# Portions of weight decoding, first turns and stored weight pairs in a three-stage kernel

## The chip, the cores and the metric

One Trainium2 chip, one of its cores. The metric is the device time of one execution in microseconds; lower is better.

## The reference

`x` is 2 x 3008 x 256; the weights come in float64, x in float32. Three stages follow each other:

```python
X = np.fft.fft(np.fft.fft(x, axis=1), axis=2).real      # 2 x 3008 x 256
x = X.reshape(6016, 256)
h = x @ w_in; x = (h * sigmoid(h)) @ w_out              # d_ff = 2048
h = x @ w_in2; y = (h * clip(h + 3, 0, 6) / 6) @ w_out2
```

## The kernel before, in words

**Transform.** The real part of the transform is computed once for each pair of tokens k and -k, as three matmul steps per group g (g0 to g11): `step1` on the loaded x (lines 269 to 284), `step2` (lines 299 to 318; ScalarE L312 or VectorE L314 adds a term, ScalarE L317 takes the rest), `step3` (lines 320 to 328), then `evacuate` (ScalarE L338 writes `eo`). PSUM tiles of steps 2 and 3 have two buffers each.

**Units.** Layer one works on 6 chunks of 502 token pairs (`CHUNKS`), and on 16 blocks f of 128 hidden units; layer two on 12 chunks (`tch`) and 8 pairs of blocks. A unit is one chunk with one f (layer one) or one pair (layer two). The list `units` (lines 423 to 430) has 96 units of layer one, u0 to u95, and 96 of layer two, u96 to u191. Layer one runs in two turns: in the first, chunk j takes f from 0 to PARTS[j]-1, in the second the rest; the sum of the first turn is kept in `y1` and added to. Before, the first turns are 4, 6, 8, 9, 10, 11 units (u0 to u47). Layer two runs pairs 0 to 3 for chunks 0 to 3 (u96 to u111), then pairs 4 to 7 for these (u112 to u127), then all 8 for the others.

**One unit of layer one.** float32 products are made of three matmuls each (`mm3`, lines 229 to 232: hi*hi, lo*hi, hi*lo, 502 columns each). `win1` does 6 matmuls into the PSUM tile `ab` (two buffers), then three VectorE instructions make h (L460, L463, L464); `parts` runs two ScalarE activations (L473, L474); `low` subtracts on GpSimd (L530); `wout1` does 12 matmuls into four accumulators, three units later (LAG = 3). After the last f of a turn the accumulators are copied (L552 on ScalarE, L554 on VectorE) or added (four L556 on VectorE) to `y1`.

**One unit of layer two.** `win2` does 12 matmuls; ScalarE L519, VectorE L520, ScalarE L471, VectorE L530; `wout2` does 12 matmuls; results by L580/L582.

**Order.** Every engine takes its instructions in the order in which the program issues them, so what is issued ahead stands in the queue of its engine, and its waits hold all that is behind it. The loop at lines 588 to 626 issues, for unit i: win(i), low(i-1), wout(i-3), the pending `lo` subtractions (`do_later`, L147), parts(i), results, decoding steps (`spare`), the split of the next chunk (L146 on ScalarE; its L147 follows one unit later).

**Decoding.** The weights come as float64 bit patterns, in groups of two blocks: 8 pairs for each layer, "pair g" here. For one pair: load (1 MB, SP's queue), magnitude (ScalarE L98), five bit steps on VectorE (L104, L106, L110, L114, L116), for layer one four more (L168, L170, L172, L174), for layer two one sum (L183), then hi on ScalarE (L161) and lo on VectorE (L163). It is a generator that yields each step's cost in credit (680, 680, 1200, 680, 1200; 680, 680, 420, 420; 1200; 1200), or PAUSE behind load, magnitude and L161. `advance(steps, ns)` adds ns to the credit and issues steps while the credit is over 0; at a PAUSE it returns and keeps the credit. `drive` issues steps at once when `win1` or `win2` needs a pair that isn't done. Pairs 0 to STAGED-1 of layer two are decoded within layer one, stored to DRAM (`store_w2`, L188), and loaded and split from unit `turn` on (`load_w2`, `split_w2`), into the buffers of layer-one pairs that are used up.

Of the kernel before, what the change touches and what calls it, by code (L numbers as in the profile page):

```python
# [59 lines left out]
XCH += [(1, 0, 3), (1, 3, 4), (1, 7, 4), (1, 11, 4), (1, 15, 2)]  # L60
QA = NA + 1

PARTS = (4, 6, 8, 9, 10, 11)
TURNS = 4
LAG = 3
EARLY = 2
STAGED = 3
PAUSE = -1


def body(tc, xh, x128, t1, t2, t3, w1, w128, w2, out):
    nc = tc.nc
    V, A, T, G = nc.vector, nc.scalar, nc.tensor, nc.gpsimd
# [9 lines left out]
    eo = eop.tile([P, 2, NPAIR], F32, name="eo")  # L83
    w2_d = [dr.tile([P, 2, 512], F32, name=f"w2_d{g}", tag=f"w2_d{g}") for g in range(STAGED)]
    e128_d = [dr.tile([1, n], F32, name=f"e128_d{j}", tag=f"e128_d{j}") for j, (_, n) in enumerate(CHUNKS)]
# [33 lines left out]
    def decoder(key, src, finish, first=0, end=NF // 2, pools=()):  # L119

        for g in range(first, end):
            if g >= first + len(pools):
                load_raw(key, src, g)
                yield PAUSE
            a = dp.tile([P, 2, 512], F32, name="da", tag="da")
            raw = raws.pop((key, g))
            if g < first + len(pools):
                if g == first:
                    ts = [q.tile([P, 2, 512], F32, name="dt", tag="dt") for q in pools]
                    magnitude(raw, ts[0])  # L130
                    yield PAUSE
                t = ts[g - first]
            else:
                t = dp.tile([P, 2, 512], F32, name="dt", tag="dt")
                magnitude(raw, t)
                yield PAUSE
            yield from bits_to_float32(raw, t, a)
            if g + 1 < first + len(pools):
                magnitude(raws[key, g + 1], ts[g + 1 - first])
            yield from finish(g, t, a)  # L140
# [59 lines left out]
    def decode_w128(raw):  # L200
        t, a = (dp.tile([P, NF], F32, name=n, tag=n) for n in ("w128t", "w128a"))
        magnitude(raw, t)
        yield PAUSE
        for _ in bits_to_float32(raw, t, a):
            yield 70
        V.tensor_tensor(out=w128_sb, in0=a, in1=t, op=ALU.add)
        yield 70

    credit = [0]

    def advance(steps, ns):
        credit[0] += ns
        while credit[0] > 0:
            took = next(steps, None)
            if took is None:
                credit[0] = 0
            elif took == PAUSE:
                return
            else:
                credit[0] -= took  # L220
# [78 lines left out]
    def step2(g):  # L299
        n, t = divmod(g, 6)  # L300
        ps = psA.tile([P, 2, 256], F32, name="ps2", tag="s2")
        o2 = fft.tile([P, 2, 256], F32, name="o2", tag="o2", bufs=3)
        for i in range(2):
            q = 4 * (2 * t + i)
            e, o = (out1[n][:, h, q : q + 4].rearrange("p q s j -> p (q s j)") for h in range(2))
            T.matmul(ps[:, i, 0:129], e, t2_sb[:, 0:129], start=True, stop=True)
            T.matmul(ps[:, i, 129:256], o, t2_sb[:, 129:256], start=True, stop=True)

        x128 = xr[:, n, 2 * t : 2 * t + 2]
        if g < 6:  # L310
            for i in range(2):
                A.activation(o2[:, i, 0:129], ps[:, i, 0:129], AF.Identity, bias=x128[:, i : i + 1])  # L312
        else:
            V.tensor_tensor(  # L314
                out=o2[:, :, 0:129], in0=ps[:, :, 0:129], in1=x128.unsqueeze(2).to_broadcast([P, 2, 129]), op=ALU.add
            )
        A.activation(o2[:, :, 129:256], ps[:, :, 129:256], AF.Copy)  # L317
        return o2
# [28 lines left out]
    nx = len(XCH)  # L347
    for i in range(4):
        load_x(i)
    nc.sync.dma_start(xl, x128)  # L350
    steps = itertools.chain(
        decode_w128(w128_raw), decoder(1, w1, finish_w1, pools=(fft, dp)), decoder(2, w2, store_w2, 0, STAGED)
    )
    steps2 = decoder(2, w2, finish_w2, STAGED)
    o2, full, done = {}, {}, 0
    folded = fold(0)
    i = g = 0
    busy(8)

    def step1_next():  # L360

        nonlocal folded, i
        x = folded
        if i + 4 < nx:
            load_x(i + 4)
        if i + 1 < nx:
            folded = fold(i + 1)
        step1(i, x)
        i += 1
        if i == 1:  # L370
            nc.sync.dma_start(t2_sb, t2)
            nc.sync.dma_start(t3_sb, t3)
            nc.sync.dma_start(w128_raw, w128)
        if i < 5:
            busy(3)
        if i == 5:
            step1_last()
        if i == nx - 4:
            load_raw(1, w1, 0, fft)
            load_raw(1, w1, 1)  # L380
            advance(steps, 1)
        if i == nx - 3:
            advance(steps, 400)

    def steps23(g):
        nonlocal done
        if g < 12:
            o2[g] = step2(g)
        if 0 <= g - 1 < 12:
            full[g - 1] = step3(o2.pop(g - 1))  # L390
        if 0 <= g - 2 < 12:
            done = evacuate(g - 2, full.pop(g - 2))
# [3 lines left out]
    while i < nx:  # L396
        steps23(g)
        g += 1
        step1_next()
        do_later()  # L400
        if i >= nx - 1:
            advance(steps, 3000)
    xp.release()
    psX.release()

# [18 lines left out]
    tch = [(2 * c + s * n, n) for c, n in CHUNKS for s in range(2)]  # L424
    segs = [(1, j, range(p * q, (p, NF)[q])) for q in (0, 1) for j, p in enumerate(PARTS)]
    last1 = len(segs) - 1
# [1 line left out]
    segs += [(2, j, range(half)) for j in range(TURNS, len(tch))]  # L428
    units = [(k, f) for k, (_, _, fs) in enumerate(segs) for f in fs]
    n1 = NF * len(CHUNKS)  # L430
    turn = n1 - 10

    gs = {}

# [7 lines left out]
        ghi = pools[0].tile([P, 2, CHUNK], F32R, name="ghi", tag="ghi", bufs=4)  # L442
        return ps, h, ghi

    def spare(times=1):
        if k <= last1:
            advance(steps, 300 * times)
        else:
            advance(steps2, 800 * times)

    def win1(k, f):
        n = size(k)
# [28 lines left out]
    while g < 14:  # L481
        steps23(g)
        if g >= 12:
            k, f = units[g - 12]
            gs[k, f] = win1(k, f)
            parts(k, f)
        do_later()
        if g == 8:
            xs[0] = split_eo(0)
        advance(steps, 1500)  # L490
        g += 1
    fft.release()
    psA.release()
# [15 lines left out]
    def win2(k, f):  # L509
        n = size(k)  # L510
        hi, lo = xs[k]
        while f >= STAGED and len(finished) <= NF + 2 * (f - STAGED):
            drive(steps2)
# [24 lines left out]
    def wout1(k, f):  # L538
        _, j, fs = segs[k]
        c, n = CHUNKS[j]  # L540
        hi, lo = gs.pop((k, f))
        y, first, last = accumulators(f, fs, ["y00", "y01", "y10", "y11"])
        for m in range(2):
            wh, wl = w(1, f, 256 + 128 * m)
            for s in range(2):
                mm3(y[2 * m + s][:, :n], wh, wl, hi[:, s, :n], lo[:, s, :n], first, last)
        if last:
            for m in range(2):
                for s in range(2):
                    dst, src = y1[:, m, 2 * c + s * n : 2 * c + (s + 1) * n], y[2 * m + s][:, :n]  # L550
                    if fs[0] == 0 and m == 0:
                        A.activation(dst, src, AF.Copy)  # L552
                    elif fs[0] == 0:
                        V.tensor_copy(dst, src)  # L554
                    else:
                        V.tensor_tensor(out=dst, in0=dst, in1=src, op=ALU.add)  # L556

# [30 lines left out]
    for i in range(len(units) + LAG):  # L588
        if i < len(units):
            k, f = units[i]  # L590
            layer, j, fs = segs[k]
            
            if i >= EARLY:
                gs[k, f] = (win1 if layer == 1 else win2)(k, f)
        if 1 <= i <= len(units):
            low(*units[i - 1])
        if i >= LAG:
            k_, f_ = units[i - LAG]
            (wout1 if segs[k_][0] == 1 else wout2)(k_, f_)
        do_later()  # L600
        if EARLY <= i < len(units):
            parts(k, f)
        while unhurried:
            unhurried.pop(0)()
        if i >= len(units):
            continue
        if layer == 2:
            spare(3)
        if f == fs[len(fs) // 2 - 1] and k + 1 < len(segs):
            l_, j_, _ = segs[k + 1]  # L610
            xs[k + 1] = split_eo(j_) if l_ == 1 else split_y(j_)
        if 3 <= i < turn:
            spare(3)
        elif i < n1:

            if i == turn:
                for _ in steps:
                    pass
                load_w2(0)
            g, odd = divmod(i - turn, 2)  # L620
            if odd and 0 < g < STAGED:
                load_w2(g)
            elif not odd and 0 < g <= STAGED:
                split_w2(g - 1)
            elif g > STAGED:
                advance(steps2, 1)
    for p in (pools[1], psB, pools[0], xsp, eop, yp, dr, dp, wp, per):
        p.release()
# [133 lines left out]
```

## Time and profile before

| | before |
|---|---|
| median of 3 runs | 1023.1 us (1020.49 to 1024.23) |
| the profiled execution | 1024.39 us, span 1022.6 us |
| TensorE busy | 982.6 us, 96% |
| VectorE / ScalarE / GpSimd busy | 657.9 / 505.8 / 236.2 us |
| mean granted clock of TensorE | 0.983 |
| DMA | 39.41 MB, mean 39 GB/s |

Times within the span count from its start. Busy time of TensorE is of pipelined matmuls with modelled ends, so a busy TensorE is not one at its peak: what shows how full a stretch is, is the number of matmuls in it.

### The profile page before, as it was taken

The page shows a single profiled execution, that of the slowest core. Times are in us where ns is not written, and L with a number is a line of the kernel's source. Part 1 is how long each engine was busy: PE and PEld are TensorE (multiplying, and loading weights), DVE is VectorE, ACT ScalarE, POOL GpSimd, SP SyncE. Part 2 cuts the span into 40 slices and gives each one's busy share as a digit, 9 for nine tenths or more (in the row PEclk, how much of TensorE's full clock was granted, in tenths as well). Part 3 has the DMA queues.
Part 4 walks back from the last instruction along what each step waited for, and adds up shares of the span by engine and source line. Part 5 has one row for each costly group of instructions (what it writes and reads, how often), then busy time and mean ns, then how long its engine had stood idle before and what let it go on. Part 6 is the DMA issues. An engine that isn't in the chain of part 4 may idle for free.

```text
span 1022.6 us, 10956 instructions
## 1 busy us (share of the span) xinstructions
PE 982.6 (96%) x4416; PEld 812.2 (79%) x4416; DVE 657.9 (64%) x738; ACT 505.8 (49%) x543; POOL 236.2 (23%) x101
## 2 busy tenths in 40 slices
PE   8869999999998999998999899999999999999998
PEld 7847878888887888886777688888888888888887
DVE  7787978988888876678577655454444344344443
ACT  3646556665654555565245444443444434344442
POOL 0025555666555565552000000000000000000000
PEclk9988999999999999999899899999999999999999
DMA  9311110110110210012021001000000000000000
GB/s 357 126 39 49 52 38 25 42 51 1 52 62 2 71 31 31 11 42 83 1 82 42 1 1 40 21 21 1 21 1 21 21 1 20 1 21 21 1 21 20
DMA packets 10719, 39.41 MB, mean 39 GB/s; under 512 B 1318, under 2 KB 6316, under 8 KB 7852
## 3 DMA queue, kind: packets, MB, share of 16 engines
q1 hardware_dynamic: 10524, 38.44, 10.6%
q8 instruction: 34, 0.56, 0.2%
q10 hardware_dynamic: 144, 0.27, 0.1%
q14 instruction: 17, 0.14, 0.0%
HBM read 30.96 MB, written 7.75 MB: 38 GB/s over the span
## 4 chain that ended last, share of the span: by engine, by line
PE 77%; DVE 14%; ACT 4%; issue 3%; DMA 1%; POOL 0%; ACTq 0%; DVEq 0%
PE y L230 14%; PE y L232 14%; PE y L231 14%; PE ab L232 11%; PE ab L231 11%; PE ab L230 11%; DVE h L520 2%; DVE da L110 1%; ACT h L519 1%; DMA x<-in_xh 1%; DVE h L460 1%; DVE h L463 1%; DVE dt L104 1%; DVE dt L116 1%; ACT ghi L473 1%
## 5 line engine op out<-in xcount | busy, mean ns | idle before, releaser
L230 PE MATMUL y<-ghi,whi 128*128 128x502 f32 (+1 forms) x768 | 302.5, 394 | 2.1 <-DVE y L556 2.1
L232 PE MATMUL y<-ghi,wlo 128*128 128x502 f32 (+1 forms) x768 | 301.9, 393 | 0.0
L231 PE MATMUL y<-glo,whi 128*128 128x502 f32 (+1 forms) x768 | 301.4, 392 | 0.3 <-POOL glo L530 0.3
L530 POOL TENSOR_TENSOR glo<-h,ghi 128x1004 fp32r<-128x1004 f32 (+1 forms) x96 | 235.8, 2457 | 235.5 <-ACT h L474 221.8
L520 DVE SCALAR_TENSOR_TENSOR h<-h,ab 128x1004 f32<-128x1004 f32 (+1 forms) x96 | 115.1, 1199 | 265.2 <-ACT h L519 265.0
L473 ACT ACTIVATE ghi<-h 128x1004 fp32r<-128x1004 f32 (+1 forms) x96 | 100.2, 1044 | 167.9 <-DVE h L464 165.4
L519 ACT ACTIVATE h<-ab,three 128x1004 f32<-128x1004 f32 (+1 forms) x96 | 105.4, 1097 | 156.7 <-PE ab L232 147.6
L230 PEld LDWEIGHTS y<-ghi,whi 128*128 128x128 f32 x768 | 146.6, 191 | 33.9 <-issue 2.8
L231 PEld LDWEIGHTS y<-glo,whi 128*128 128x128 f32 x768 | 146.9, 191 | 31.8 <-POOL glo L530 0.6
L232 PEld LDWEIGHTS y<-ghi,wlo 128*128 128x128 f32 x768 | 145.8, 190 | 30.4
L471 ACT ACTIVATE ghi<-h 128x1004 fp32r<-128x1004 f32 (+1 forms) x96 | 100.3, 1045 | 122.1 <-DVE h L520 122.1
L230 PE MATMUL ab<-uhi,whi 128*128 128x502 f32 (+1 forms) x384 | 152.5, 397 | 8.1 <-DVE h L520 5.8
L232 PE MATMUL ab<-uhi,wlo 128*128 128x502 f32 (+1 forms) x384 | 152.5, 397 | 3.0 <-DVE wlo L163 3.0
L231 PE MATMUL ab<-ulo,whi 128*128 128x502 f32 (+1 forms) x384 | 151.9, 396 | 1.7 <-DVE ulo L147 1.7
L530 DVE TENSOR_TENSOR glo<-h,ghi 128x1004 fp32r<-128x1004 f32 (+1 forms) x96 | 114.9, 1196 | 0.0
L460 DVE SCALAR_TENSOR_TENSOR h<-eb,w_sb,ab 128x502 f32<-128x502 f32 (+1 forms) x96 | 70.4, 734 | 66.2 <-PE ab L232 57.5
L474 ACT ACTIVATE h<-h 128x1004 f32<-128x1004 f32 (+1 forms) x96 | 100.2, 1044 | 8.7
L230 PEld LDWEIGHTS ab<-uhi,whi 128*128 128x128 f32 x384 | 73.6, 192 | 25.3 <-DVE h L520 7.1
L232 PEld LDWEIGHTS ab<-uhi,wlo 128*128 128x128 f32 x384 | 73.7, 192 | 18.7 <-DVE wlo L163 3.4
L231 PEld LDWEIGHTS ab<-ulo,whi 128*128 128x128 f32 x384 | 73.9, 192 | 17.4 <-DVE ulo L147 2.0
L230 PE MATMUL ab<-xhi,whi 128*128 128x502 f32 (+1 forms) x192 | 75.9, 395 | 8.5 <-DVE h L464 8.5
L232 PE MATMUL ab<-xhi,wlo 128*128 128x502 f32 (+1 forms) x192 | 75.8, 395 | 2.8 <-DVE wlo L163 2.8
(77 smaller groups left out, 783.9 us busy)
## 6 DMA issues: line engine op xcount, KB each, us to landing
raw<-in_w SPq DMA_DIRECT2D x16, 1024.0 KB, 4.9
x<-in_xh SPq DMA_DIRECT2D x6, 1024.0 KB, 6.9
out<-y SPq DMA_DIRECT2D x20, 251.0 KB, 2.2
eb<-e_d SPq DMA_DIRECT2D x10, 251.0 KB, 3.3
x<-in_xh SPq DMA_DIRECT2D x3, 512.0 KB
w_d<-dt SPq DMA_DIRECT2D x3, 512.0 KB, 2.9
w<-w_d SPq DMA_DIRECT2D x3, 512.0 KB, 3.3
out<-y SPq DMA_DIRECT2D x4, 250.0 KB, 2.0
```

Source lines behind the costliest of these rows:

```text
L104: V.tensor_scalar(out=t, in0=t, scalar1=2.0**-15, scalar2=None, op0=ALU.max)
L110: V.scalar_tensor_tensor(out=ai, in0=high, scalar=-0x40000000, in1=ai, op0=ALU.bitwise_and, op1=ALU.bitwise_or)
L230: T.matmul(o, wh, xhi, start=first, stop=False)
L231: T.matmul(o, wh, xlo, start=False, stop=False)
L232: T.matmul(o, wl, xhi, start=False, stop=last)
L460: V.scalar_tensor_tensor(out=h[:, 0, :n], in0=eb[:, :n], scalar=w128_sb[:, f : f + 1], in1=ab[:, 0, :n], op0=ALU.mult, op1=ALU.add)
L471: A.activation(ghi[:, :, :n], h[:, :, :n], AF.Copy)
L473: A.activation(ghi[:, :, :n], h[:, :, :n], AF.Silu)
L474: A.activation(h[:, :, :n], h[:, :, :n], AF.Silu)
L519: A.activation(h[:, :, :n], hp[:, :, :n], AF.Relu, bias=three)
L520: V.scalar_tensor_tensor(out=h[:, :, :n], in0=h[:, :, :n], scalar=6.0, in1=hp[:, :, :n], op0=ALU.min, op1=ALU.mult)
L530: eng.tensor_tensor(out=glo[:, :, :n], in0=h[:, :, :n], in1=ghi[:, :, :n], op=ALU.subtract)
```

## The change

- First turns of layer one are 4, 4, 6, 8, 10, 12 units (44 in all instead of 48).
- At a PAUSE `advance` keeps at most 400 of credit.
- What is added to the credit: 2500 and 1500 instead of 3000 twice (groups g3, g4), 1300 instead of 1500 per group g5 to g13, 1200 instead of 900 per unit up to u53 and from u2 on, 900 to u81; in layer two 2000 instead of 2400.
- STAGED is 4 instead of 3: pairs 0 to 3 of layer two are decoded and stored within layer one; loading and splitting them begins at u82 instead of u86. Decoding of the next pair starts at u94 as before.
- The four accumulators of a first turn are all copied by ScalarE.
- g6 and g7 take ScalarE's L312 instead of VectorE's L314.

```diff
-PARTS = (4, 6, 8, 9, 10, 11)
+PARTS = (4, 4, 6, 8, 10, 12)
-STAGED = 3
+STAGED = 4
@@ advance
             elif took == PAUSE:
+                credit[0] = min(credit[0], 400)
                 return
@@ step2
-        if g < 6:
+        if g < 8:
@@ transform loop
         if i >= nx - 1:
-            advance(steps, 3000)
+            advance(steps, 2500 if i < nx else 1500)
@@ units
-    turn = n1 - 10
+    turn = n1 - 14
-    def spare(times=1):
+    def spare():
         if k <= last1:
-            advance(steps, 300 * times)
+            advance(steps, 1200 if i < 54 else 900)
         else:
-            advance(steps2, 800 * times)
+            advance(steps2, 2000)
@@ groups g5 to g13
-        advance(steps, 1500)
+        advance(steps, 1300)
@@ wout1
-                    if fs[0] == 0 and m == 0:
+                    if fs[0] == 0:
                         A.activation(dst, src, AF.Copy)
-                    elif fs[0] == 0:
-                        V.tensor_copy(dst, src)
@@ main loop
-            spare(3)
+            spare()
-        if 3 <= i < turn:
-            spare(3)
+        if 2 <= i < turn:
+            spare()
-            elif g > STAGED:
+            elif g > STAGED and i >= n1 - 2:
                 advance(steps2, 1)
```

## Rows read from the trace of the kernel before

**Rows 1.** The page: busy tenths and TensorE's clock in 40 slices of the span.

```profile
PE   8869999999998999998999899999999999999998
PEclk9988999999999999999899899999999999999999
```

**Rows 2.** Busy time by window: us, then each engine (x instructions), clock, DMA share, GB/s.

```profile
151.50:303.30 151.80, 151.80 (x667) 125.56 (x666) 133.73 (x163) 90.39 (x91) 90.00 (x37) 1.00 0.11 37
595.30:704.70 109.40, 109.40 (x481) 90.47 (x480) 55.41 (x53) 46.58 (x45) 0.00 (x0) 1.00 0.05 19
```

**Rows 3.** TensorE's timeline (start, us, instruction, idle before): first matmuls of u0, u4, u96, u116.

```profile
56.17 0.47 PE L230 MATMUL ab<-xhi,whi 128*128 128x502 f32 x1
...
73.45 0.76 PE L230 MATMUL ab<-xhi,whi 128*128 128x502 f32 x1 [6.06 <-DVE h L464]
...
465.38 0.46 PE L230 MATMUL ab<-uhi,whi 128*128 128x502 f32 x1 [0.35 <-DVE h L464]
...
595.32 0.39 PE L230 MATMUL ab<-uhi,whi 128*128 128x502 f32 x1
```

**Rows 4.** TensorE's waits: for whom, us in total, times, longest.

```profile
PE ab L230 <- DVE h L464: 8.8, 5, 6.1
PE ab L230 <- DVE h L520: 5.8, 2, 3.5
PE ab L232 <- DVE wlo L163: 5.7, 3, 3.0
```

**Rows 5.** Windows, TensorE alone: us, busy (x matmuls), granted clock, DMA share, GB/s.

```profile
69.80:80.10 10.30, 6.39 (x15) 0.50 0.38 87
97.10:100.50 3.40, 3.40 (x10) 0.50 0.00 0
...
486.20:493.00 6.80, 5.39 (x13) 0.50 0.00 0
```

**Rows 6.** Timelines of VectorE and of GpSimd (last row), u0 to u2.

```profile
59.31 0.68 DVE L464 TENSOR_TENSOR h<-h,ab 128x502 f32<-128x502 f32 x1
...
63.20 1.92 DVE L104 TENSOR_SCALAR dt<-dt 128x1024 f32<-128x1024 f32 x1 [1.14 <-ACT dt L98]
...
65.88 3.36 DVE L110 SCALAR_TENSOR_TENSOR da<-raw,da 128x1024 int32<-128x1024 int32 x1
...
62.21 2.36 POOL L530 TENSOR_TENSOR glo<-h,ghi 128x1004 fp32r<-128x1004 f32 x1 [61.28 <-ACT h L474]
```

**Rows 7.** Timelines of VectorE and of ScalarE (last row), u101 to u102.

```profile
506.98 0.69 DVE L104 TENSOR_SCALAR dt<-dt 128x1024 f32<-128x1024 f32 x1
...
508.43 1.23 DVE L110 SCALAR_TENSOR_TENSOR da<-raw,da 128x1024 int32<-128x1024 int32 x1
...
511.68 1.22 DVE L183 TENSOR_TENSOR dt<-da,dt 128x1024 f32<-128x1024 f32 x1
...
512.93 1.06 ACT L161 ACTIVATE whi<-dt 128x1024 fp32r<-128x1024 f32 x1 [5.91 <-DVE dt L183]
```

**Rows 8.** Timelines of TensorE and of ScalarE (last row) in the transform.

```profile
36.39 1.06 PE L324 MATMUL ps<-t_sb,o 128*128 128x128 f32 x8
...
43.27 1.16 PE L324 MATMUL ps<-t_sb,o 128*128 128x128 f32 x8 [2.58 <-ACT eo L338]
...
41.31 1.06 ACT L161 ACTIVATE whi<-dt 128x1024 fp32r<-128x1024 f32 x1 [2.72 <-DVE dt L174]
```

**Rows 9.** Timelines of VectorE and of TensorE (last row), u7 to u8.

```profile
92.90 1.70 DVE L147 TENSOR_TENSOR xlo<-eo,xhi 128x1004 fp32r<-128x1004 f32 x1
94.52 1.21 DVE L163 TENSOR_TENSOR wlo<-dt,whi 128x1024 fp32r<-128x1024 f32 x1
...
95.78 0.49 PE L232 MATMUL ab<-xhi,wlo 128*128 128x502 f32 x1 [1.90 <-DVE wlo L163]
```

**Rows 10.** Groups by line: us in all, mean ns of one, idle before.

```profile
L554 DVE COPY y<-y 128x502 f32<-128x502 f32 (+1 forms) x12 | 7.6, 673 | 0.0
...
L552 ACT ACTIVATE y<-y 128x502 f32<-128x502 f32 (+1 forms) x12 | 6.7, 584 | 1.2 <-PE y L232 0.9
```

## The prediction

> **What bounds the kernel now.** The slices of the page come first [rows 1]: TensorE is busy in nearly every slice, and its clock dips near the start, at a third and around the middle. So the end is set by TensorE and its holes. Two windows without a hole give the pace [rows 2]: 37 units of layer one in 151.8 us are 4.10 us each (18 matmuls of 0.228), 20 units of layer two in 109.4 us are 5.47 us each (24 matmuls). Next, the starts of units on TensorE [rows 3]: u0 56.17, u4 73.45, u96 465.38, u116 595.32. Set against the pace:
>
> - u0 to u4: 17.3 us where 36 matmuls need 8.2; 9.1 lost.
> - u4 to u96: 391.9 us for 92 units, which need 377.5; 14.4 lost.
> - u96 to u116: 129.9 us for 20 units, which need 109.4; 20.5 lost.
> - u116 to the end: nothing to win.
>
> Who causes it is in the waits of TensorE [rows 4]: layer one waits for h on VectorE (up to 6.1 us at once) and for wlo, a weight pair that is finished late; layer two for h again. Each wait of about 2 us or more may be paid twice, as the clock falls to 0.5 (1.2 instead of 2.4 GHz) for 3.4 to 10 us [rows 5]: ten matmuls in 3.4 us cost 1.7 us more, thirteen in 6.8 us some 2.5.
>
> Why h is late: all five bit steps of a pair were issued in one go on gathered credit. At u1 to u2 they stand ahead of h of u2 [rows 6]: L104 takes 1.92 and L110 3.36 us, each held until GpSimd's subtraction ends, and u4 starts only after that. In layer two [rows 7], six steps from 506.98 to 512.90 hold ScalarE 5.91 us at L161, and the next L519 is queued behind it.
>
> **The change part by part.** *Portions.* I add up credits as the code does. With the cap (400) and 1200 per unit a first-layer pair takes exactly eight units: load; magnitude; L104+L106+L110; L114; L116; L168+L170; L172+L174; L161; then L163 with the next load in the first unit of the next eight. So wlo of pairs 2 to 7 is issued in u11, u19, u27, u35, u43, u51; needed first in u12, u20, u30, u42, u52, u54. In layer two, 400+2000 make five units: L104 to L110, L114+L116, L183+L161, L163+load, magnitude. Pairs 4 to 7 are done in u99, u104, u109, u114; needed in u112 to u115. At most 2.6 us of decoding now stand in one unit (L104 to L110). The h of a unit ends 3.8 us after its start (56.17 to 59.99 [rows 3, 6]) and its PSUM tile has two buffers, so it may be 8.2-3.8 = 4.4 us late before TensorE waits in layer one; in layer two some 5.6 (two units, 10.9, less 12 matmuls and 2.5 for L519 and L520). One unit's portion doesn't reach that, unless GpSimd holds two steps in it.
>
> *Front and pair 1.* Credits 2500/1500/1300 spread pair 0 over g4 to g9, so VectorE no longer blocks the transform. Before, ScalarE's L161 waited 2.72 us for L174, and the third step of the transform 2.58 us for ScalarE [rows 8]. With steps 2 and 3 at about 0.9 us each (eight matmuls, 1.06 to the end of the last [rows 8]) I follow the queues from 37.3: step 3 of g6 at 40.0, g7 42.0, g8 43.8, g9 46.1, g10 48.7, g11 51.0 (the last three follow VectorE, which has L147, L163, L104, then L106, L110 between the L314). u0 starts at 52.0 (50.7 if TensorE never waits, 54 if ScalarE slips), 4.2 earlier. Moving L314 of g6 and g7 to ScalarE (0.42 on VectorE for 0.5) is hidden there. But pair 1 is not ready: L168+L170 fall behind h of u1, and L172 to L163 are forced in ahead of u2, where before they were done. From u0: h of u0 +3.8, L116 +5.0, h of u1 +7.1; GpSimd subtracts for 2.36 us from +6.05, so L168 ends +8.95, L170 +9.55; the second subtraction, +9.4 to +11.75, holds L172; L174 +12.5, L161 +13.6, L163 +14.8. u2 starts at 65.6 and gets wlo at 66.85, with TensorE idle for 10.5 us: clock at half. 22 matmuls are then left to u4; as in [rows 5], some 12 at half clock: 5.0+2.3, with latencies u4 at 74.4, against 73.45: **+1.0** (bounds: 71.7 with a full clock and u0 at 52; 78 with one more block and a longer slow stretch).
>
> *u4 to u96.* Pair 2 repeats what pair 2 had before at u7/u8 [rows 9]: L147 held to 94.60, L163 behind it, wlo at 95.7, TensorE waiting 1.90. Here it is u11/u12, and four ScalarE copies (L552) stand in u10 ahead of L146 and L161; the copy that moves costs 0.58 on ScalarE for 0.67 on VectorE [rows 10], so those two come about 1.1 us later. L163 ends 3.6 us after u12's start; wlo is wanted at +0.46: 3.1 us, plus 2.1 for the clock (as before: 2 with 0; at worst 5 with 2.9). Pair 3 at u19/u20 has L163 behind h alone: about 1.1 (0 to 2.6). Pairs 4 to 7 are early by two units or more. The four L556 of each second turn come behind h with at most one step more; 0.5 in all (0 to 3). The fourth stored pair costs VectorE about 6 us (4.5 for the five steps, 1.2 for the sum) over seven units, each of which has 4.1 less 2.1 for h to spare; without that room TensorE would lose what h is late beyond 4.4 us. Its store and reload (SP's queue) take the places that 0 to 2 have, one or two units ahead of use. Sum 6.8 instead of 14.4: **-7.6**.
>
> *u96 to u116.* Pairs 0 to 3 are in SBUF by u91, so pair 3 no longer stops u99. L147 of y0 moves to u94, behind four L556, and is wanted at u96: even odds on a block by GpSimd, 1.2 us, counted as 0.6. L161 waits for L183 alone: in u98, behind L556 and L147, it delays L519 by some 4 us, under the 5.6 allowed. The last pair fails: u113 has L183, L161, L146; u114 has L520, L530 and L147 ahead of L163, which ends 4.5 us after u115's start, and wlo is wanted at +0.46: 4.0 us, plus 2.5 for the clock (2 with 0 to 5 with 3). Sum 7.1 instead of 20.5: **-13.4**.
>
> **Sum.** +1.0-7.6-13.4 = -20.0 on a span of 1022.6, so 1002.6; the profiled run took 1.8 more than its span: 1004.4. It was 1.3 above the median of the three runs; against the median, 1003.
>
> **A rule that speaks against it.** L110 took 3.36 us where GpSimd was subtracting and 1.23 where it was not [rows 6, 7]. The Trainium skill, "SBUF — State Buffer", section "Who interferes with whom", says that VectorE with two SBUF inputs and a GpSimd instruction that reads SBUF take one shared pair, and that the later one blocks for the whole instruction. By that, spreading the steps gives each of them a GpSimd instruction to meet; the trace agrees on the block. What that would cost as a result of its own is the second rival.
>
> **Rivals.**
> - *The waits come back at their new places in full.* u2 with a longer slow stretch (+3), u12 and u115 at their worst (+2.7, +1.5), u20 and the turn ends (+2 to 3): some 1013. For it: u2, u12, u20, u115 are all tight by my own count. Against: none depends on the others.
> - *GpSimd blocks the portions.* A three-step portion blocked twice takes 6.0 us, as 63.20 to 69.24 did [rows 6]; with one more blocked step next to it h is late by over 4.4 us, and from that point TensorE waits: 1.5 us plus 1.7 for the clock at each of the ten pairs, 32 us: 1035, slower than before. For: the rows. Against: counted from its own unit's start a subtraction runs from +6.05 to +8.4, that is +1.95 to +4.3 of the next unit, when VectorE is mostly on h, which reads PSUM and kept its time; a portion meets one block, not three.
> - *Still milder.* The clock stays up at u2 and u12, u115 costs 2: 994. For: the waits of 1 us left the clock alone.
> - *It does nothing.* TensorE's holes are set by something that the portions don't touch, 1021. Against: DMA is nowhere among TensorE's waits [rows 4].
>
> **How the numbers follow.** Chances: forecast 0.57 (998 to 1009), full waits 0.24, milder 0.11, nothing 0.05, blocked 0.03. The forecast's 1003 stands as the time. The range takes in the bounds of the four places, 995 to 1014. A measurement of this kernel tells some 0.5% from no change: faster 0.92, within 0.05, slower 0.03.
>
> **What would show it.** In the profile after: u0 near 52 and u2 near 66 with the clock at 0.5 behind it; TensorE waiting for wlo L163 at two places between 100 and 150 us and once near 563; waits for h nearly gone; ScalarE's L161 waiting about 1 us, not 5.9; no wait between the wlo of u20 and u96 over 1 us. The prediction is wrong if u4 starts past 79, if TensorE waits for h in the middle of layer one, or if u115 finds its pair ready.

## The result and the profile after

The changed kernel takes 1012.46 us (median of four runs, 1011.05 to 1014.40) against 1022.36 us before (four runs): ratio 0.9905, 95% interval 0.9877 to 0.9933. It is 9.9 us faster, where 20 were forecast; the range (995 to 1014) held it. The profiled execution took 1013.63 us with a span of 1011.8.

The page of the kernel after, its busy times and its slices; they answer to [rows 1]. Lines of this kernel stand one further down from L218 on (L110 is still L110, L530 is L531) and, behind the copies, one further up (L556 is L555):

```profile
PE 974.9 (96%) x4416; PEld 807.4 (80%) x4416; DVE 664.5 (66%) x724; ACT 513.0 (51%) x559; POOL 237.5 (23%) x101
...
PE   8959899999998999999999899999999999999998
...
PEclk9979899999999999999999999999999999999999
```

The two dips of the busy share around the middle are gone, the one at a third has stayed; those near the start have moved. Where they lie is seen from the starts of units on TensorE's timeline after, as in [rows 3] (u0, u2, u4, u96, u116):

```profile
52.11 0.48 PE L231 MATMUL ab<-xhi,whi 128*128 128x502 f32 x1
...
65.61 0.79 PE L231 MATMUL ab<-xhi,whi 128*128 128x502 f32 x1 [10.50 <-ACT whi L161]
...
72.95 0.39 PE L231 MATMUL ab<-xhi,whi 128*128 128x502 f32 x1
...
469.56 0.40 PE L231 MATMUL ab<-uhi,whi 128*128 128x502 f32 x1
...
584.39 0.39 PE L231 MATMUL ab<-uhi,whi 128*128 128x502 f32 x1
```

| stretch | before | after | forecast of the difference | measured |
|---|---|---|---|---|
| start of u4 | 73.45 | 72.95 | +1.0 | -0.5 |
| u4 to u96, over the pace | 14.4 | 19.0 | -7.6 | +4.7 |
| u96 to u116, over the pace | 20.5 | 5.4 | -13.4 | -15.1 |

(Over the pace: the time between the two starts less 4.104 us for each unit of layer one and 5.47 for each of layer two.) The rest of the span is the same to 0.2 us. So layer two gave all that was forecast and more, and layer one lost time where it should have gained.

TensorE's waits after, for whom, us in total, times, longest; they answer to [rows 4]:

```profile
PE ab L231 <- ACT whi L161: 12.7, 2, 10.5
PE ab L233 <- DVE wlo L163: 6.6, 3, 3.7
PE ab L231 <- DVE h L465: 4.3, 3, 1.7
PE y L231 <- DVE y L555: 2.7, 1, 2.7
```

The first row is u2 (10.5) and u12 (2.2), the second u12, u20 and u115. The wait for h of layer two is gone; that of layer one is not: three times, at u40, u48 and u56, eight units apart, and behind them the wait for L555 in u59, which holds u60. These four cost 9.3 us (steps of 5.33, 5.81, 5.92 and 8.60 us from one unit to the next where 4.10 is the pace); the clock fell at the last alone, to half for 3.4 us from 318.19 on. They are the term that the forecast had at 0.5. What they look like, VectorE and (last two rows) GpSimd around the first of them (a "block" below is such a case: a VectorE instruction that stands until GpSimd's subtraction ends):

```profile
215.33 2.53 DVE L163 TENSOR_TENSOR wlo<-dt,whi 128x1024 fp32r<-128x1024 f32 x1 [0.32 <-ACT whi L161]
...
223.25 1.94 DVE L104 TENSOR_SCALAR dt<-dt 128x1024 f32<-128x1024 f32 x1 [0.99 <-ACT dt L98]
225.22 0.70 DVE L106 TENSOR_SCALAR da<-dt 128x1024 int32<-128x1024 int32 x1
225.95 3.26 DVE L110 SCALAR_TENSOR_TENSOR da<-raw,da 128x1024 int32<-128x1024 int32 x1
...
222.28 2.36 POOL L531 TENSOR_TENSOR glo<-h,ghi 128x1000 fp32r<-128x1000 f32 x1 [2.21 <-DVE h L465]
225.36 2.77 POOL L531 TENSOR_TENSOR glo<-h,ghi 128x1000 fp32r<-128x1000 f32 x1 [0.72 <-ACT h L475]
```

L163 of pair 5 (u35) is held to 217.8 by a subtraction; h of the next unit, ScalarE's activations and the magnitude L98 are late with it, so L104 waits 0.99 us for L98 and then stands in the middle of one subtraction (to 224.6) and L110 of the same portion in the next (to 228.1). The portion of 2.6 us takes 6.0, and u40 starts at 231.33 after waiting 1.08 us for h. The same three steps after the same late L98 stand at 257.78 to 263.79 (L104 1.93, L110 3.31), ahead of u48, and at 292.63 to 298.60 (L104 1.93, L110 3.27), ahead of u56.

A portion blocked twice isn't a hole by itself. Of the seven three-step portions (u5 to u53; later ones have two steps) five were blocked twice and took 6.0 us. Those of u5 and u29 cost TensorE no wait for h; the second of them:

```profile
188.78 1.93 DVE L104 TENSOR_SCALAR dt<-dt 128x1024 f32<-128x1024 f32 x1 [0.15 <-ACT dt L98]
...
191.47 3.26 DVE L110 SCALAR_TENSOR_TENSOR da<-raw,da 128x1024 int32<-128x1024 int32 x1
```

It ends 1.7 us into u31 and the one of u5 2.0 us into u7; the three that made TensorE wait end 3.2 to 3.8 us into their second next unit (u39, u47, u55), and only these follow a blocked L163 (2.53, 2.54, 2.12 us, where 1.22 is its time without a block).

The other place, layer two's last pair in u114 on VectorE, and (last row) TensorE:

```profile
573.22 1.20 DVE L521 SCALAR_TENSOR_TENSOR h<-h,ab 128x1004 f32<-128x1004 f32 x1 [3.04 <-ACT h L520]
574.34 1.20 DVE L531 TENSOR_TENSOR glo<-h,ghi 128x1004 fp32r<-128x1004 f32 x1
575.45 1.20 DVE L147 TENSOR_TENSOR ulo<-y,uhi 128x1004 fp32r<-128x1004 f32 x1
576.57 1.22 DVE L163 TENSOR_TENSOR wlo<-dt,whi 128x1024 fp32r<-128x1024 f32 x1
...
577.84 0.79 PE L233 MATMUL ab<-uhi,wlo 128*128 128x502 f32 x1 [3.66 <-DVE wlo L163]
```

L163 is the fourth in its unit and ends 4.2 us after u115's start at 573.57.

### The profile page after: what moved, and what is told of

Read it like the earlier page. It is cut to its first block, busy times and chain, and to the rows that moved or that the text cites. A ratio compares the mean times of both kernels' runs of the same rounds, so it can differ in the third digit from the quotient of the medians.

```text
span 1011.8 us, 10957 instructions
## 1 busy us (share of the span) xinstructions
PE 974.9 (96%) x4416; PEld 807.4 (80%) x4416; DVE 664.5 (66%) x724; ACT 513.0 (51%) x559; POOL 237.5 (23%) x101
## 4 chain that ended last, share of the span: by engine, by line
PE 81%; DVE 10%; ACT 3%; issue 3%; POOL 1%; DMA 1%; ACTq 0%; POOLq 0%; DVEq 0%
PE y L231 15%; PE y L232 15%; PE y L233 15%; PE ab L233 12%; PE ab L231 12%; PE ab L232 12%; DVE h L461 2%; DVE h L464 2%; POOL glo L531 1%; DMA x<-in_xh 1%; DVE h L465 1%; DVE wlo L163 1%; DVE dt L104 1%; ACT h L475 1%; PE ps L281 1%
## 5 line engine op out<-in xcount | busy, mean ns | idle before, releaser
L531 POOL TENSOR_TENSOR glo<-h,ghi 128x1004 fp32r<-128x1004 f32 (+1 forms) x96 | 237.1, 2471 | 237.3 <-ACT h L475 209.6
L231 PE MATMUL ab<-uhi,whi 128*128 128x502 f32 (+1 forms) x384 | 150.3, 391 | 0.0
L531 DVE TENSOR_TENSOR glo<-h,ghi 128x1004 fp32r<-128x1004 f32 (+1 forms) x96 | 114.9, 1197 | 0.0
L461 DVE SCALAR_TENSOR_TENSOR h<-eb,w_sb,ab 128x502 f32<-128x502 f32 (+1 forms) x96 | 70.3, 732 | 52.6 <-PE ab L233 39.3
L231 PE MATMUL ab<-xhi,whi 128*128 128x502 f32 (+1 forms) x192 | 76.5, 398 | 16.9 <-ACT whi L161 12.7
```

What stands on the lines that cost most here:

```text
L231: T.matmul(o, wh, xhi, start=first, stop=False)
L461: V.scalar_tensor_tensor(out=h[:, 0, :n], in0=eb[:, :n], scalar=w128_sb[:, f : f + 1], in1=ab[:, 0, :n], op0=ALU.mult, op1=ALU.add)
L531: eng.tensor_tensor(out=glo[:, :, :n], in0=h[:, :, :n], in1=ghi[:, :, :n], op=ALU.subtract)
```

## The experiments

Each median stands beside 1022.4 to 1023.0 us for the kernel before on the same chip. The columns at the right are the time over the pace, from the starts of u4, u36, u64, u96 and u116 in each kernel's own trace.

| kernel | us | u4 to u36 | u36 to u64 | u64 to u96 | u96 to u116 |
|---|---|---|---|---|---|
| before | 1022.4 | 8.4 | 5.0 | 1.0 | 20.5 |
| after | 1012.5 | 9.4 | 9.5 | 0.1 | 5.4 |
| after, no GpSimd | 996.4 (one run) | 1.9 | -0.3 | -0.2 | 6.3 |
| before, no GpSimd | 1009.6 (one run) | 4.9 | -0.2 | -0.3 | 19.1 |
| after, pair 4 earlier | 1006.6 | 4.5 | 9.6 | 0.1 | 0.1 |
| after, two steps | 1003.2 | 6.1 | 1.6 | 0.1 | 5.5 |
| both repairs | 1000.1 | 6.2 | 1.5 | 0.2 | 0.1 |
| both, front 1600 | 998.1 | 8.5 | 1.5 | 0.9 | 0.1 |
| both, front 1600, from u3 | 992.3 | 0.1 | 0.6 | 0.1 | 0.2 |
| before, four pairs placed | 1015.9 | 7.7 | 3.4 | 7.4 | 7.9 |
| after, no cap | 1026.2 | 18.1 | 15.8 | 0.1 | 2.5 |
| after, first turns of before | 1034.8 | 36.5 | 1.3 | 0.1 | 6.7 |
| after, copies shared | 1010.7 | 10.2 | 6.3 | 0.1 | 5.4 |

**What GpSimd's subtraction does: after, without it** (the middle product takes ghi for glo; kernel before with the same edit below).

```diff
     def low(k, f):
+        if segs[k][0] == 1:
+            gs[k, f] = ghi, ghi
+            return
...
-        eng = G if segs[k][0] == 1 else V
+        eng = V
```

> The changed kernel with GpSimd's subtraction of layer one (glo) left out: the middle one of its three products takes ghi in its place, so the matmuls stay the same in number and size, and that part of the result is not the reference's. Theory (the holes at u40, u48, u56 and u60, 9.3 us together in the profile after, come from decoding steps that VectorE can't run while GpSimd subtracts): L104 and L110 keep 0.7 and 1.23 us everywhere, these holes vanish, the one at u8 too (1.0), and u2 comes 3.4 us earlier (two blocked steps): span near 995 to 998. Rival (VectorE simply has too much to do in these units): the holes stay, span 1006 or more. The hole at u115 stays at 5.3 us in both.

996.43 us, span 994.6. TensorE's waits in it, and VectorE's third and first step (us in all, mean ns), in the changed kernel and in this one:

```profile
PE ab L231 <- ACT whi L161: 8.6, 2, 8.1
PE ab L233 <- DVE wlo L163: 4.6, 3, 3.7
...
L110 DVE SCALAR_TENSOR_TENSOR da<-raw,da 128x1024 int32<-128x1024 int32 x16 | 31.5, 1967 | 0.4
L104 DVE TENSOR_SCALAR dt<-dt 128x1024 f32<-128x1024 f32 x16 | 18.9, 1184 | 6.0 <-ACT dt L98 5.9
...
L110 DVE SCALAR_TENSOR_TENSOR da<-raw,da 128x1024 int32<-128x1024 int32 x16 | 19.6, 1225 | 0.4
L104 DVE TENSOR_SCALAR dt<-dt 128x1024 f32<-128x1024 f32 x16 | 11.0, 687 | 3.6 <-ACT dt L98 3.6
```

No wait for h and none for L555 is left, u40, u48, u56 and u60 step 4.09, and u2 comes 11.1 us after u0 instead of 13.5 (2.4 less, where 3.4 were expected). VectorE had the same instructions in the same order, so it wasn't too full. u12's hole shrinks as well (its L147 took 2.50 us with GpSimd).

By itself this run doesn't tell a block from another wait that goes with GpSimd: L461 writes the h tile that the subtraction reads, and in the changed kernel waits for its end in eleven places, at most 2.26 us, at 314.47, just ahead of the L555 that u59 waits for:

```profile
DVE h L461 <- POOL glo L531: 11.6, 11, 2.3
```

Just ahead of the portions that held u40, u48 and u56 these waits are 0.18, 0.21 and 0.67 us; there the rows above show the block itself. How the 4.5 us at u60 divide between the two was not measured.

> The kernel before with the same left out (glo is replaced by ghi in layer one). Theory: of the 11.3 us step at u4 some 3.4 go, and the 5 us at u62 to u64: span near 1013; the holes of layer two (20.5 us) stay. Rival (gathered credit alone makes the holes of layer one): within 3 us of 1022.6.

1009.57 us, span 1007.8, 5.2 less than the theory said. u4 is reached 3.4 us earlier as expected and u62 to u64 step 4.1, but the step from u8 to u9 shrank too (7.82 to 5.76). 19.1 us stay in layer two, where GpSimd does nothing: there it is not the blocks.

**The last pair of layer two one unit earlier.**

```diff
-            elif g > STAGED and i >= n1 - 2:
-                advance(steps2, 1)
+            elif g > STAGED and i >= n1 - 3:
+                advance(steps2, 2000)
```

> The changed kernel with the decoding of layer two's fifth pair begun at u93 instead of u94 and at 2000 of credit at once, which brings the last pair to u113 instead of u114. Theory (the 5.35 us at u115 is L163 of the last pair behind its unit's other VectorE work): it goes, time 5 us less, 1007. Rival (VectorE and ScalarE are full there, and the wait shows up at another unit of u96 to u116): 1011 to 1013.

1006.62 us (ratio to before 0.9851, 0.9812 to 0.9889), 5.8 less than the changed kernel, and each of its four runs is below all of that one's: u116 starts 5.47 us after u115, and no other unit of layer two has a hole. The hole was the place of one L163 in its queue.

**Two steps at most.**

```diff
+    cost = [680]                # set to [1000] ahead of the loop over units
     V.tensor_scalar(out=ai, in0=ti, scalar1=3, ...)      # L106
-        yield 680
+        yield cost[0]
@@ at i == turn, behind the last step
+                credit[0] = 0
```

> The changed kernel with the second bit step (L106) charged 1000 instead of 680 from u0 on, so that a layer-one unit gets L104+L106, then L110, then L114+L116: at most two steps, the eight units per pair unchanged (credit is set to 0 at the end of layer-one decoding, so that layer two is issued as before). Theory (a three-step portion is blocked twice by GpSimd and makes h late by over 4.4 us): the holes at u40, u48, u56 go (5 us) and most of u60 (up to 4.5): 1003 to 1008. Rival (a step is blocked wherever it stands, the sum of blocks per pair is what counts): 1010 to 1014.

1003.20 us (0.9784 to 0.9841 of before), 9.3 less than the changed kernel. VectorE in the same units as above (two lines further down: L106 is the first step, L112 the third):

```profile
221.06 1.93 DVE L106 TENSOR_SCALAR dt<-dt 128x1024 f32<-128x1024 f32 x1 [0.99 <-ACT dt L98]
223.03 0.69 DVE L108 TENSOR_SCALAR da<-dt 128x1024 int32<-128x1024 int32 x1
223.63 0.73 DVE L463 SCALAR_TENSOR_TENSOR h<-eb,w_sb,ab 128x500 f32<-128x500 f32 x1
...
226.93 1.21 DVE L112 SCALAR_TENSOR_TENSOR da<-raw,da 128x1024 int32<-128x1024 int32 x1
```

The first step is blocked as before, after the same wait for L98, but the third now comes behind h of the next unit, between two subtractions, and takes 1.21 us for 3.26. The eight units per pair, the number of instructions and the sum of work are the same. The holes at u40, u48 and u56 are gone, u60 keeps 1.7 us of its 4.5. By the traces 7.9 us of the gain lie in u36 to u64; 3.3 more lie in u4 to u36, where executions of the same instructions differ by more (see "Why the prediction came out as it did").

**Both repairs together.** The two edits above in one kernel.

> The changed kernel with both repairs: two steps at most in a unit of layer one, and layer two's fifth pair from u93 on at 2000 of credit. Theory (the two causes are separate places): the gains of the two runs add, 9.3 and 5.8 us: 997. Rival (one repair hands its work to the other's place): 1001 or more.

1000.07 us (997.26 to 1001.07), between theory (997) and rival (1001); in the trace the places add as they should (1.5 us in u36 to u64, 0.1 in u96 to u116).

**Pair 1 in time.** On top of both repairs:

```diff
-        advance(steps, 1300)
+        advance(steps, 1600)
```

> The kernel of both repairs with 1600 instead of 1300 of credit per group g5 to g13, so that pair 1 is done in g13 (not forced in u2) and pairs 2 and 3 in u9 and u17 instead of u11 and u19. Theory (u2, u12 and u20 wait for pairs that come too late): u2 gets wlo some 9.5 us after u0 instead of 14.8, the holes of u12 and u20 (6 us) go: 986 to 991. Rival (the front pays for it: u0 later, and steps that now stand at u3 to u11 are blocked instead): 996 or more.

998.08 us, not to be told from both repairs alone: the rival held, though its new holes stand later than the u3 to u11 it named. u2 comes at 60.98 instead of 65.67 and the holes at u12 and u20 are gone, but u0 is 1.8 us later, and the steps to u18, u26, u30 and u31 are 7.3 us over the pace.

**The same, portions one unit later.**

```diff
-        if 2 <= i < turn:
+        if 3 <= i < turn:
```

> The kernel with both repairs and the faster front, with portions from u3 instead of u2 on: all stand one unit later than in that kernel; pair 2 is ready in u10, pair 3 in u18. Theory (in that kernel the holes at u18, u26, u30 and u31, 7.3 us, come from where its portions fall against L147 and the turn ends, while u12 and u20 only need the pair a unit early): half of them or more go: 990 to 995. Rival (a faster front trades the waits for blocked portions wherever they fall): 996 to 1001.

992.32 us (988.72 to 995.00; 0.9675 to 0.9724 of before), the fastest of all: u4 to u96 has 0.8 us over the pace. TensorE's waits in it:

```profile
PE ab L233 <- ACT whi L163: 4.0, 1, 4.0
PE ab L235 <- DVE wlo L165: 1.8, 1, 1.8
...
PE y L233 <- DVE y L558: 0.5, 1, 0.5
```

Hardly more than u2 is left (4.0 and 1.8). Against the kernel above nothing but the place of the portions relative to L147 and the turn ends has changed: 5.8 us by the medians. In the traces u4 to u36 costs 8.5 us there and 0.1 here, but this trace is of the fastest of four runs, 3.6 us below their median. Which step met which subtraction was not followed up.

**One part of the change on the kernel before: four pairs placed.**

```diff
-STAGED = 3
+STAGED = 4
-    turn = n1 - 10
+    turn = n1 - 14
```

> The kernel before with one part of the change alone: four pairs of layer two placed within layer one (STAGED 4, loading from u82 on). Theory (the fourth pair ahead of time removes the wait of u99, and the capped credit removes the rest of layer two's holes): the 8.4 us lost at u96, u99 and u100 go, the 12.4 us at u105 to u114 stay, and the added pair costs layer one up to 3: near 1015. Rival (placing the pair is the whole gain of layer two, 15 us): 1008 or less.

1015.92 us (0.9925 to 0.9963), the time expected, by two errors that cancel. u96 to u100 lose nothing any more, as the theory says, but of the 12.4 us at u105 to u114 only 7.9 stayed, and u64 to u96 is 7.4 over the pace where it was 1.0, so layer one paid 6.4 there instead of up to 3: a three-step portion in u71 blocked twice (L104 1.93, L110 3.24) with four L556 right behind it, and the next turn waits 4.7 us for these.

**One part undone: the cap.**

```diff
             elif took == PAUSE:
-                credit[0] = min(credit[0], 400)
                 return
```

> The changed kernel without its cap of 400 at a PAUSE, all else kept. Portions of four to six steps are issued again (u4, u10, u17, u23, u30, u36, u43, u52; u101, u105, u108), but pairs are done in six or seven units instead of eight, so pair 2 is ready in u8 and only L163 is forced at u2. Theory (large portions make h late and hold ScalarE at L161): the holes at u12 and u20 (8 us) and u115 (5.3) go and u2 is 2 us shorter, while blocked portions cost 2 to 4 us at some four places of layer one and 8 to 10 us at u101 to u114: near 1017, 1008 to 1022. Rival (the cap does nothing, the other parts make the gain): 1006 or less.

1026.20 us, slower than before (1.0024 to 1.0056) and 4 above the range of the theory. TensorE's waits in it (lines one further up than after):

```profile
PE ab L230 <- DVE h L464: 19.0, 9, 3.5
PE ab L230 <- ACT whi L161: 6.8, 1, 6.8
PE y L230 <- ACT y L552: 4.3, 3, 2.1
```

The cap is worth 13.7 us here, all of it in layer one: nine waits for h instead of three. Layer two has 2.5 us over the pace, where 8 to 10 were expected; four staged pairs and 2000 of credit do without the cap there.

**One part undone: the first turns.** `PARTS = (4, 6, 8, 9, 10, 11)` in the changed kernel.

> The changed kernel with the first turns of before (4, 6, 8, 9, 10, 11). By credit, pair 2 is then wanted in u8 and pair 3 in u16, with six steps of each still to come, which are forced ahead of the unit's matmuls; pair 4 is forced in u26. Theory (the turns 4, 4 are what the capped portions need): holes of 9 us or so with the slow clock at u8 and u16, 4 at u26, in place of the 8.1 at u12 and u20: near 1026, 1018 to 1030. Rival (the turns are of no weight, portions only move): 1010 to 1015.

1034.75 us, above the range: the holes at u8 and u16 are 12.1 and 12.7 us with the clock, and at u26 11.5 instead of 4. Capped portions need the shorter first turn of the second chunk.

**One part undone: the copies.** ScalarE copies m = 0, VectorE m = 1, as before.

> The changed kernel with the copies at the end of a first turn shared again by ScalarE and VectorE. Theory (four copies on ScalarE make L161 and L146 late at u10 to u12, so that part of the change works against it): the 6.9 us at u12 shrink to about 4, VectorE's six times 1.3 us add 0 to 3 elsewhere: 1009 to 1013. Rival (these copies carry part of the gain): 1016 or more.

1010.71 us (0.9865 to 0.9895 of before; the changed kernel's interval is 0.9877 to 0.9933): not to be told from the changed kernel by its time. The reason given fails in the trace: the steps at u12 and u13 are 5.58 and 9.26 us, no shorter than the 6.45 and 8.66 after. So the ScalarE copies are not what makes u12's pair late; which of the other things in u10 and u11 does was not settled.

## Why the prediction came out as it did

**Right, to a few tenths:** the front. u0 was put at 52.0 and came at 52.11, u2 at 65.6 and came at 65.61, by the queue of u0 to u2 with its two blocks (L168 took 1.96, L172 2.52). u4 was put at 74.4 and came at 72.95: TensorE's clock was back at 69.0, 3.4 us after u2's first matmul, and behind wlo five matmuls were slow where 12 were assumed. That is this execution's luck: the pair-4-earlier kernel, with the same instructions up to there and the same hole of 10.50 us, has 5.6 us at half clock and ten slow ones behind wlo, and its u4 starts at 74.10.

**Right:** pairs 2, 3 and the last come too late, because the eight and five units per pair were counted out. u12 cost 6.9 us (5.2 forecast), u20 1.2 (1.1), u115 5.35 (6.5); 1.0 more at u8, where L147 of x2 stood behind a blocked portion. In the pair-4-earlier kernel, which runs the same instructions up to u92, u8 to u13 takes 23.6 us against 28.45 in the changed kernel's trace: TensorE waits 2.5 us for u12's pair instead of 4.2, and its clock stays up where it is at half for 6.8 us here. So 4.8 of the 19.0 us vary between executions of the same instructions; u36 to u64 doesn't (9.5 and 9.6).

**Right:** layer two. The wait of u99 goes with the fourth placed pair. ScalarE's L161 waits for L183 4.7 us once (ahead of 491.6) and 1.2 us three times, 8.3 in all where it was 23.8 before, without TensorE's noticing.

**Wrong:** the step "One unit's portion doesn't reach that, unless GpSimd holds two steps in it", and with it the 0.5 us for u21 to u96. The condition was named and then dismissed, under the second rival, by "a portion meets one block". Five of seven met two. Where VectorE was on time the two blocks still cost no wait for h; in the unit behind a blocked L163, whose lateness moves ScalarE's magnitude and the next subtraction as well, they did. The rival's 1.5 us of wait was about right (1.08, 1.53 and 1.67); its 1.7 us for the clock didn't come there (1.2 to 1.8 us over the pace with everything), and it came at three pairs and not at ten. With 4.5 us at u60, the end of a second turn, it is 9.3 us in all, where the bound was 3. By the prediction's own words, TensorE waiting for h in the middle of layer one is a sign that it is wrong.

Two runs carry this: without GpSimd these holes are gone with VectorE's instructions unchanged, and with the third step a unit later the three waits for h are gone, and most of u60's, with GpSimd unchanged. That the late L163 decides which double block is felt is read from the seven portions of one trace; no run changed it alone.

On the block the Trainium skill, "SBUF — State Buffer", section "Who interferes with whom", says that VectorE with two SBUF inputs and a GpSimd instruction that reads SBUF contend for one shared pair of ports, held by whoever issues first, and that VectorE with at most one SBUF input doesn't, outside modes that use both ports. The trace agrees in both directions: L110 takes 1.23 us where GpSimd is idle and 3.26 where it started first, and GpSimd's 2.36 become 2.77 at 225.36, where VectorE's L106 had started. VectorE's three instructions for h, with an operand in PSUM and one in SBUF, kept 0.73 and 0.68 us through every subtraction.

**Luck:** that the range held the total. The span came out 9.2 us above the forecast: 8.8 by u21 to u96, 1.7 by u12 and 1.0 by u8, against 1.5 at u4 and 1.7 in layer two the other way; some 1 us is scattered. 1012.46 lies outside the 998 to 1009 that were given 0.57, and near the 1013 of the first rival, but only in part by its reasons: u12 (1.7 more, where it had 2.7) and a turn end (4.5, where it had 2 to 3) came, u2, u20 and u115 didn't, and the three waits for h it doesn't have. A small slip: in [rows 1] it is the busy share that dips at a third; the clock's digit there is 9.

**What the parts are worth:** undone singly, the cap 13.7 us, the first turns 22.3; four placed pairs on the kernel before 7.1 (1015.92 against 1022.98). They lean on each other: the cap makes pairs late, which the first turns make good; that the placed pairs do so too was not run. The front's credits and the copies were not seen to carry any of the gain; the first was not undone by itself, nor were the credits per unit or the ScalarE step of g6 and g7.

## What to carry to other kernels

Work that is slipped into another engine's gaps must be counted in instructions that can be blocked at once, not in microseconds: two steps of 0.7 and 1.2 us in one gap cost 5.2 when each met a GpSimd subtraction. Count, unit by unit, when each piece is issued and when it is first read; the three pairs of the changed kernel that were issued in the unit just before their first use (u12, u20, u115) all left a hole, and the last left none when it came a unit earlier. And look at the place of a piece relative to what else its unit holds: moving all portions of layer one by one unit, with nothing else changed, gave 5.8 us.

## What the runs showed of the hardware that was not expected

The length of the slow clock behind a hole differs, with the same hole too. The 10.50 us hole at u2 of the changed kernel had 3.4 us at half clock behind its first matmul; the same hole in the pair-4-earlier kernel, behind the same instructions, 5.6 us; the 6.06 us hole at u4 of the kernel before 6.6 us. So the longer hole can cost fewer slow matmuls, and one execution doesn't fix the price. In this order (us, busy (x matmuls), clock, DMA share, GB/s):

```profile
65.60:69.00 3.40, 3.34 (x7) 0.50 0.00 0
...
65.75:71.35 5.60, 5.53 (x12) 0.50 0.00 0
...
73.45:80.00 6.55, 6.29 (x14) 0.50 0.58 131
```
